# Attention interleaved with a two-matmul MLP: other gaps for the score, value and mixing steps of a pair of heads

## The chip, the cores and the metric

One Trainium2 chip, one of its cores. The metric is the device time of one execution in microseconds (us), the median of the timed runs. TensorE does the matmuls (PE in the profile, its weight loads PEld), VectorE (DVE), ScalarE (ACT) and GpSimd (POOL) do the rest, and SyncE (SP) issues most DMA transfers. All values are float32; the MLP's matmuls use two-part operands (a high part in the chip's fp32r type and the rest), three matmuls for each product.

## The reference, cut to what matters

```python
# q, k, v: (8 batches, 8 heads, 576, 64)
scores = matmul(q, k.T) / sqrt(64)               # masked: block of 64 of the key <= that of the query
attn   = exp(scores - max) / (sum + 1e-9)
x      = matmul(attn, v)                         # -> (8, 576, 512), heads side by side
u      = x + ((x.T @ U) @ V).T                   # mixing along the sequence, rank 32
ch     = relu(u @ w_ch1) @ w_ch2                 # 512 -> 2048 -> 512
y      = u + ch
gate   = sigmoid(causal_conv5(y, conv_w))
out    = (gate * (y @ w_val)) @ w_out
```

## The kernel before, in words

The 4608 rows (8 batches of 576) are cut into nine groups of 512 for the MLP. A group takes 16 steps (`NF`), one for each 128 of the 2048 hidden columns. A step is an `emit_h1` (12 matmuls into one PSUM bank, then ACT makes the high part `hh`, L1015, and DVE the low part `hl`, L1016) and an `emit_o` of the step before (12 matmuls into four accumulator banks, L1036). The order of TensorE's instructions is that of the program (`manual_schedule`); the other engines' instructions are put in order by a planner, by the program's order and by when their data is ready in its own model, and each engine then runs its queue strictly in that order.

Attention is done for pairs of heads, four pairs to a batch, 32 in all. The first eight pairs (batches 0 and 1) are done in another way (`slot`) before and during group 0, and pairs 8 and 9 by `tick` without places in group 0. The change is about pairs 10 to 31, which run between the MLP's matmuls in groups 1 to 6. After each half of a step the MLP calls `gap(kind)`: kind 0 in the middle of h1, 1 at its end, 2 in the middle of o, 3 at its end, so a group has 64 gaps. In a gap the generator `attention()` is asked on; it emits instructions until it says that it has to wait for a later gap. `until` is that wait: a part of pair p is due at the group's first count plus `POS0` plus the pair's place in the group times a period plus the part's own offset, and two parts with TensorE work don't share a gap (`used`).

What a pair does, with its names:

- S: score matmuls, `emit_s_piece` (L420), four pieces, both heads at once, a PSUM bank for each head and piece, copied to SBUF by ACT (L425). Pieces 0 and 1 (16 matmul instructions) are the first score stay, pieces 2 and 3 (8) the second.
- maxima: `emit_max_a`, `_b`, `_c` on DVE (L618 to L664); subtraction `emit_sub` (L671) on DVE; exp `emit_exp` (L687) on ACT; sums `emit_sum_a` on POOL (L694, L696) and `emit_sum_b` on DVE (L703).
- V: values, `emit_pv` (L729, sums L739), two banks, copied by ACT (L741); from the second bank DVE takes the sums as well (L746), turns their reciprocals (L749), and POOL multiplies (L750).
- T: transposes `mix_T` (L789, L797), G: `mix_G` (L805), H: `mix_H` (L828), which together add the rank-32 mixing, store u to HBM and put its two parts into the MLP's operand. `prep_t` (L398, L399) transposes the next pair's q and k on DVE.

Score, value, T, G and H banks and those of h1 come from one pool tag, "a", with four banks (`ABUF`) in turn; the accumulators hold the other four.

The places before, as offsets from a pair's first gap, for group 1 (12 gaps a pair, five pairs 10 to 14) and for the later groups (16 gaps, four pairs):

```python
    PAIR1 = 3 * NP + 3
    POS0 = 6
    PLACES = (
        (12, {"S0": 0, "m0": 2, "S2": 4, "H0": 5, "H1": 6, "T0": 7, "T1": 8, "V": 9, "m1": 10, "G": 11, "x": 11}),
        (16, {"S0": 0, "m0": 2, "S2": 4, "H0": 5, "H1": 6, "T0": 7, "T1": 8, "V": 9, "m1": 11, "G": 14, "x": 15}),
    )
```

S0 and S2 must besides fall on a gap of kind 2 or 3. V at pair p's offset 9 is that of pair p - 1; T and G are of pair p - 2, H of pair p - 3; "x" is where the second head's softmax is emitted (the first head's follows H). A batch's last H lets the group that needs it begin (`pace[2]`); where it hasn't come, the stream is run on at once (`FLUSH`). H's second piece, for a group two ahead, is put off (`later`) until that group's operand buffer is free.

Of the kernel before, what the change touches and what calls it, by code (L numbers as in the profile page):

```python
# [22 lines left out]
def attn_moe_gate_kernel(ctx: ExitStack, tc: tile.TileContext, q, k, v, U, V, w1, w2, wval, convw, wout, out):  # L23
# [62 lines left out]
    PAIR1 = 3 * NP + 3  # L86
    POS0 = 6
    PLACES = (
        (12, {"S0": 0, "m0": 2, "S2": 4, "H0": 5, "H1": 6, "T0": 7, "T1": 8, "V": 9, "m1": 10, "G": 11, "x": 11}),
        (16, {"S0": 0, "m0": 2, "S2": 4, "H0": 5, "H1": 6, "T0": 7, "T1": 8, "V": 9, "m1": 11, "G": 14, "x": 15}),  # L90
    )
# [749 lines left out]
    at_gap = {"kind": 0, "count": 0, "used": -1}  # L841
    begun = {}

    def until(n, what, kinds=None):

        p = n // 2
        if p < PAIR0:
            return
        g, i = (1, p - PAIR0) if p < PAIR1 else (2 + (p - PAIR1) // NP, (p - PAIR1) % NP)
        period, place = PLACES[g > 1]  # L850
        busy = what[0] in "SHTVG"
        while at_gap["kind"] != FLUSH:
            c = at_gap["count"]
            if g in begun and c >= begun[g] + POS0 + period * i + place[what] and (kinds is None or at_gap["kind"] in kinds) and not (busy and at_gap["used"] == c):
                break
            yield WAITS
        if busy:
            at_gap["used"] = at_gap["count"]

    def tick(n, mixed, last=B * NP):  # L860
# [7 lines left out]
        if old and not half:  # L868
            load_v(n - 2)
            load_v(n - 1)  # L870
        for i in range(4):
            if new and not half:
                if n < 2 * PAIR0:
                    emit_s_piece(n // 2, i)
                elif i % 2 == 0:
                    yield from until(n, f"S{i}", (2, 3))
                    emit_s_piece(n // 2, i)
                    emit_s_piece(n // 2, i + 1)
            if old and half and i == 0:
                yield from until(n, "V")  # L880
                emit_pv(pn, 0)
                emit_pv(pn, 1)
            if i == (0 if half else 3) and new:
                emit_corners(n)
                emit_max_a(n)
            if i == (2 if half or n < 2 * PAIR0 else 1) and NQ <= n - 1 < NH:
                yield from until(n, f"m{half}")
                emit_sum_b(n - 1)
            yield
# [5 lines left out]
        if half:  # L895
            yield from until(n, "x")
# [9 lines left out]
    def mixing(at, first, last=B * NP):  # L906

        for step, delay in ((mix_H2, H0), (mix_G, G0), (mix_T, T0)) if last == NP else ((mix_H2, HPOS), (mix_G, GPOS), (mix_T, TPOS)):
            pn, off = divmod(at - delay, 4)
            if off == 0 and first <= pn < last:  # L910
                if URG and pn == NP - 1:
                    with tc.high_priority():
                        for _ in step(pn):
                            pass
                else:
                    part = step(pn)
                    for j in range(2):
                        if j:
                            yield
                        if last > NP:  # L920
                            yield from until(at // 2 + DEPTH, "G" if step is mix_G else f"{'T' if step is mix_T else 'H'}{j}")
                        if next(part, WAITS) == WAITS:
                            break
                yield step is mix_H2 and pn % NP == NP - 1

    def attention():
# [8 lines left out]
        for n in range(NQ, NH + DEPTH + HPOS // 2):  # L935
            if n == NQ + EARLY:
                yield True
            yield from tick(n, 2 * NP)

# [266 lines left out]
    def gap(kind):  # L1206
# [5 lines left out]
        if begun and not pace[2]:  # L1212
            pace[0] = 99.0
# [14 lines left out]
    for s in range(NS + LAG):  # L1228
# [6 lines left out]
        if f == 0 and g < B:  # L1235
            while g > 0 and not pace[2]:
                pace[0] = 1.0
                gap(FLUSH)
            if g > 0:
                begun[g] = at_gap["count"]  # L1240
# [78 lines left out]
```

## Time and profile before

| | us |
|---|---|
| timed runs | 1389.58, 1389.25, 1387.07 |
| median | 1389.25 |
| profiled execution, its own time | 1385.46 |
| span of its trace | 1383.7 |
| TensorE busy | 1333.4 |
| DVE busy | 986.6 |
| ACT busy | 552.6 |
| POOL busy | 445.1 |

Mean granted clock of TensorE 0.991. The span is from the first to the last instruction; the execution's own time has 1.8 us around it. Busy time of TensorE is modelled: matmuls overlap, so that a wait can be partly covered by the record of the matmul before it. Group 1 starts at 253.9 us, group 2 at 393.7, group 3 at 517.8, group 4 at 641.8, group 5 at 765.6, group 6 at 889.4; from about 990 no attention is left, and from 1179 the last stage (values, gate and output) runs.

### The profile page before, as it was taken

What the parts mean: (1) busy time and instruction counts of PE and PEld (TensorE: products, weight loads), DVE (VectorE), ACT (ScalarE), POOL (GpSimd) and SP (SyncE); (2) the same over time, 40 slices, a digit from 0 to 9 for tenths busy, and PEclk for the clock granted to TensorE, in tenths of its full rate; (3) what the DMA queues carried; (4) which work ended last, traced back from release to release, by engine and by line L of the source; (5) the groups of instructions that cost most, each with busy time, mean ns of one, the idle gap of its engine ahead of it and who ended that gap; (6) DMA issues with size and microseconds to landing.
All of it is one profiled execution on the core that took longest, in us unless ns stands there. A gap on an engine that the chain in (4) does not pass through costs nothing.

```text
span 1383.7 us, 20054 instructions
## 1 busy us (share of the span) xinstructions
PE 1333.4 (96%) x6840; PEld 1029.5 (74%) x6840; DVE 986.6 (71%) x2085; ACT 552.6 (40%) x1210; POOL 445.1 (32%) x648
## 2 busy tenths in 40 slices
PE   6889889999999999999999999999999999999999
PEld 4667665777677777777777777778878888788887
DVE  5986789788878778777877877772235164699981
ACT  5785544333343334334433433432223122434432
POOL 3443334423343224334322422441132100624210
PEclk9999998999999999999999999999999999999999
DMA  6667785644364347435443644332375632332311
GB/s 109 159 179 209 230 263 170 140 95 115 78 135 107 93 113 155 111 92 142 104 99 96 155 105 111 102 103 88 116 206 167 154 128 99 77 107 77 107 60 62
DMA packets 257936, 173.60 MB, mean 125 GB/s; under 512 B 202149, under 2 KB 222885, under 8 KB 257834
## 3 DMA queue, kind: packets, MB, share of 16 engines
q1 hardware_dynamic: 250282, 162.58, 42.5%
q0 software_dynamic: 5184, 9.44, 4.5%
q8 instruction: 54, 0.88, 0.3%
q10 hardware_dynamic: 2368, 0.30, 0.2%
q14 instruction: 48, 0.39, 0.1%
HBM read 135.57 MB, written 36.70 MB: 125 GB/s over the span
## 4 chain that ended last, share of the span: by engine, by line
PE 59%; DVE 24%; ACT 7%; DMA 5%; issue 3%; SPq 1%; POOL 0%; ACTq 0%; DVEq 0%; POOLq 0%
PE acc L1036 18%; PE h L987 18%; PE o L1150 7%; PE val L1126 7%; PE pS L420 4%; DMA raw<-in_moe_w_ch_dram 3%; DVE hl L1016 2%; DVE mb L664 2%; PE pPV L729 2%; DVE s L671 2%; DVE r L657 2%; ACT e L687 1%; DVE wa L133 1%; DVE g L105 1%; ACT s L687 1%
## 5 line engine op out<-in xcount | busy, mean ns | idle before, releaser
L1036 PE MATMUL acc<-hh,w 128*128 128x512 f32 x1152 | 404.3, 404 | 1.6 <-DMA w<-w_s 1.6
L1036 PEld LDWEIGHTS acc<-hh,w 128*128 128x128 f32 x1152 | 218.2, 189 | 72.1 <-issue 23.4
L987 PE MATMUL h<-uh,w1hi 128*128 128x512 f32 x576 | 233.1, 405 | 1.2 <-DVE xt L830 1.0
L1036 PE MATMUL acc<-hl,w 128*128 128x512 f32 x576 | 226.7, 394 | 0.2 <-DVE hl L1016 0.2
L987 PE MATMUL h<-uh,w1lo 128*128 128x512 f32 x576 | 226.0, 392 | 0.0
L987 PE MATMUL h<-ul,w1hi 128*128 128x512 f32 x576 | 225.6, 392 | 0.0
L1016 DVE SCALAR_TENSOR_TENSOR hl<-h,hh 128x512 fp32r<-128x512 f32 x144 | 98.6, 685 | 141.3 <-ACT hh L1015 139.7
L1015 ACT ACTIVATE hh<-h 128x512 fp32r<-128x512 f32 x144 | 85.9, 597 | 242.2 <-PE h L987 241.8
L987 PEld LDWEIGHTS h<-uh,w1hi 128*128 128x128 f32 x576 | 108.8, 189 | 27.6 <-issue 1.8
L987 PEld LDWEIGHTS h<-uh,w1lo 128*128 128x128 f32 x576 | 108.7, 189 | 23.7
L1036 PEld LDWEIGHTS acc<-hl,w 128*128 128x128 f32 x576 | 109.5, 190 | 19.8 <-DVE hl L1016 0.5
L987 PEld LDWEIGHTS h<-ul,w1hi 128*128 128x128 f32 x576 | 109.0, 189 | 20.1 <-issue 0.4
L1108 DVE SCALAR_TENSOR_TENSOR gt<-yb,cw,gt 128x516 f32<-128x516 f32 (+1 forms) x144 | 115.2, 830 | 1.4
L420 PE MATMUL pS<-tq,tk 64*128 64x320 f32 (+4 forms) x576 | 99.0, 420 | 13.1 <-DVE hl L1016 10.2
L105 POOL TENSOR_TENSOR yl<-yb,yh 128x512 fp32r<-128x512 f32 (+7 forms) x64 | 66.8, 1077 | 102.7 <-ACT yh L99 102.6
L105 POOL TENSOR_TENSOR ul<-xt,uh 128x512 fp32r<-128x512 f32 (+7 forms) x64 | 60.2, 948 | 112.7 <-ACT uh L99 112.6
L420 PEld LDWEIGHTS pS<-tq,tk 64*128 64x128 f32 x576 | 52.2, 187 | 51.3 <-issue 24.6
L425 ACT COPY s<-pS 128x320 f32<-128x320 f32 (+2 forms) x128 | 59.6, 501 | 36.5 <-PE pS L420 36.5
L671 DVE TENSOR_TENSOR s<-s,mb 128x64 f32<-128x64 f32 (+4 forms) x160 | 70.6, 507 | 0.5
L694 POOL TENSOR_TENSOR m<-e 128x448 f32<-128x448 f32 x24 | 31.0, 1293 | 122.5 <-ACT e L687 117.7
L729 PE MATMUL pPV<-e,vstk 128*64 128x192 f32 (+4 forms) x384 | 70.2, 336 | 0.1
L729 PEld LDWEIGHTS pPV<-e,vstk 128*64 128x64 f32 x384 | 46.8, 137 | 24.5 <-issue 12.6
(180 smaller groups left out, 2502.9 us busy)
## 6 DMA issues: line engine op xcount, KB each, us to landing
w<-w_s SPq DMA_DIRECT2D x144, 512.0 KB, 3.5
rawq<-in_q_dram SPq DMA_DIRECT2D x128, 72.0 KB, 3.0
out_dram<-ot SPq DMA_DIRECT2D x35, 256.0 KB, 2.0
rawk<-in_k_dram SPq DMA_DIRECT2D x124, 72.0 KB, 2.9
vstk<-in_v_dram SPq DMA_DIRECT2D x68, 128.0 KB, 2.9
raw<-in_moe_w_ch_dram SPq DMA_DIRECT2D x64, 128.0 KB, 2.4
raw<-in_moe_w_ch_dram SPq DMA_DIRECT2D x16, 512.0 KB, 3.9
w_s<-wo SPq DMA_DIRECT2D x16, 512.0 KB, 4.3
```

The source lines that it names most:

```text
L105: eng.tensor_tensor(o, i, f32(h), op=ALU.subtract)
L420: pe.matmul(t[:, o:o + w], tk[me, kslice(j)], tq[me, a0:a1], start=True, stop=True)
L425: act.copy(stt[n][half_of[j]][:, d:d + o], t[:, 0:o])
L671: noted(3, vec.tensor_tensor(sv(n, j), sv(n, j), mb[:, q0[j]:], op=ALU.subtract))
L729: pe.matmul(ps[me, a0 - c0:c1 - c0], vpart(n)[:, j, :], est[n][half_of[j]][:, soff[j] + a0 - q0[j]:soff[j] + c1 - q0[j]], start=j == 0, st ...
L987: pe.matmul(ps[:, 0:n], w[:, d, fs], x[:, d, 0:n], start=(d == 0 and i == 0), stop=(d == ND - 1 and i == 2))
L1015: act.activation(hh[:, 0:n], ps[:, 0:n], AF.Relu)
L1016: latest[0] = vec.scalar_tensor_tensor(hl[:, 0:n], ps[:, 0:n], 0.0, f32(hh[:, 0:n]), op0=ALU.max, op1=ALU.subtract)
L1036: pe.matmul(acc[d][:, 0:n], w[:, wi, ds], x[:, 0:n], start=(f == 0 and i == 0), stop=(f == NF - 1 and i == 2))
L1108: vec.scalar_tensor_tensor(gt[d][:, 0:gw], y[:, d, j:j + gw], cw[:, d, j:j + 1], gt[d][:, 0:gw], op0=ALU.mult, op1=ALU.add)
L1126: pe.matmul(ps[:, 0:n], w[:, d, es], x[:, d, 0:n], start=(i == 0), stop=(i == 3 * ND - 1))
L1150: pe.matmul(ps[:m, cs], x[:, e, a:a + m], w[:, e, cs], start=(i == 0), stop=(i == 3 * ND - 1))
```

## The change

All pairs from 10 on get 16 gaps, counted through from the first gap of group 1 (`at_gap["first"]`), four pairs to a group; `POS0` is 8. `pair_tick` writes one pair's order out: offset 0 the first score stay, and the pair's loads of v (before, they were issued one pair later); 2 and 3 the H of pair p - 2; 4 the values of pair p - 1 and behind them, in the same gap, the second score stay; 6 the first head's softmax, 8 the second head's maxima, 9 the first head's sums, 10 the second head's softmax; 11 and 12 the T of pair p - 1; 13 the next pair's q and k and the second head's sums; 15 the G of pair p - 1. The kinds of the gaps are no longer asked for: offset 0, 4, 8 and 12 are gaps of kind 3 (except in a group's first step). A group starts when its batch is in `ready`.

```diff
@@ -83,12 +83,8 @@
     WAITS = 3
     FLUSH = 4
     PAIR0 = (NQ + EARLY) // 2
-    PAIR1 = 3 * NP + 3
-    POS0 = 6
-    PLACES = (
-        (12, {"S0": 0, "m0": 2, "S2": 4, "H0": 5, "H1": 6, "T0": 7, "T1": 8, "V": 9, "m1": 10, "G": 11, "x": 11}),
-        (16, {"S0": 0, "m0": 2, "S2": 4, "H0": 5, "H1": 6, "T0": 7, "T1": 8, "V": 9, "m1": 11, "G": 14, "x": 15}),
-    )
+    POS0 = 8
+    PERIOD = 4 * (NF // NP)
 
     def f32(ap):
         return ap if ap.dtype == F32 else ap.bitcast(F32)
@@ -838,24 +834,93 @@
 
     y_done = [-1]
 
-    at_gap = {"kind": 0, "count": 0, "used": -1}
-    begun = {}
-
-    def until(n, what, kinds=None):
-
-        p = n // 2
-        if p < PAIR0:
-            return
-        g, i = (1, p - PAIR0) if p < PAIR1 else (2 + (p - PAIR1) // NP, (p - PAIR1) % NP)
-        period, place = PLACES[g > 1]
-        busy = what[0] in "SHTVG"
+    at_gap = {"kind": 0, "count": 0, "used": -1, "first": None}
+    ready = set()
+
+    def until(p, off, pe_step=True):
+
         while at_gap["kind"] != FLUSH:
             c = at_gap["count"]
-            if g in begun and c >= begun[g] + POS0 + period * i + place[what] and (kinds is None or at_gap["kind"] in kinds) and not (busy and at_gap["used"] == c):
+            if at_gap["first"] is not None and c >= at_gap["first"] + POS0 + PERIOD * (p - PAIR0) + off and not (pe_step and at_gap["used"] == c):
                 break
             yield WAITS
-        if busy:
+        if pe_step:
             at_gap["used"] = at_gap["count"]
+
+    turned_to = [2 * NP]
+    mixed_to = [2 * NP]
+
+    def turning(p, t0, t1, g, n=None):
+        pn = turned_to[0]
+        turned_to[0] += 1
+        turn = mix_T(pn)
+        yield from until(p, t0)
+        next(turn)
+        yield from until(p, t1)
+        next(turn, None)
+        if n is not None:
+            yield from until(p, t1 + 1, False)
+            prep_t(n)
+            emit_sum_b(2 * p + 1)
+        yield from until(p, g)
+        for _ in mix_G(pn):
+            pass
+
+    def pair_tick(p):
+
+        a, b = 2 * p, 2 * p + 1
+        new = a < NH
+        if new:
+            yield from until(p, 0)
+            emit_s_piece(p, 0)
+            emit_s_piece(p, 1)
+            load_v(a)
+            load_v(b)
+        while mixed_to[0] <= p - 2 and mixed_to[0] < turned_to[0]:
+            pn = mixed_to[0]
+            mixed_to[0] += 1
+            for i in range(2):
+                yield from until(p, 2 + i)
+                mix_H(pn, i)
+            if pn % NP == NP - 1:
+                ready.add(pn // NP)
+        if turned_to[0] < min(p, B * NP) - 1:
+            yield from turning(p, 1, 2, 3)
+        if new or p - 1 < B * NP:
+            yield from until(p, 4)
+        if p - 1 < B * NP:
+            emit_pv(p - 1, 0)
+            emit_pv(p - 1, 1)
+        if new:
+            emit_s_piece(p, 2)
+            emit_s_piece(p, 3)
+            emit_corners(a)
+            emit_max_a(a)
+            emit_max_b(a)
+            yield from until(p, 6, False)
+            soften(a)
+            yield from until(p, 8, False)
+            emit_corners(b)
+            emit_max_a(b)
+            emit_max_b(b)
+            if p == PAIR0:
+                for i in range(2):
+                    yield from until(p, 6 + i)
+                    mix_H(mixed_to[0], i)
+                mixed_to[0] += 1
+            yield from until(p, 9, False)
+            emit_sum_b(a)
+            yield from until(p, 10, False)
+            soften(b)
+        if turned_to[0] < min(p + 1, B * NP):
+            yield from turning(p, 11, 12, 15, p + 1 if new else None)
+    def soften(n):
+        for _ in emit_max_c(n):
+            pass
+        emit_sub(n, 0)
+        emit_sub(n, 1)
+        emit_exp(n)
+        emit_sum_a(n)
 
     def tick(n, mixed, last=B * NP):
 
@@ -868,23 +933,19 @@
         if old and not half:
             load_v(n - 2)
             load_v(n - 1)
+        if n == 2 * PAIR0 - 1:
+            load_v(n - 1)
+            load_v(n)
         for i in range(4):
             if new and not half:
-                if n < 2 * PAIR0:
-                    emit_s_piece(n // 2, i)
-                elif i % 2 == 0:
-                    yield from until(n, f"S{i}", (2, 3))
-                    emit_s_piece(n // 2, i)
-                    emit_s_piece(n // 2, i + 1)
+                emit_s_piece(n // 2, i)
             if old and half and i == 0:
-                yield from until(n, "V")
                 emit_pv(pn, 0)
                 emit_pv(pn, 1)
             if i == (0 if half else 3) and new:
                 emit_corners(n)
                 emit_max_a(n)
-            if i == (2 if half or n < 2 * PAIR0 else 1) and NQ <= n - 1 < NH:
-                yield from until(n, f"m{half}")
+            if i == 2 and NQ <= n - 1 < NH:
                 emit_sum_b(n - 1)
             yield
         if new:
@@ -892,8 +953,6 @@
             if half:
                 prep_t((n + 1) // 2)
         yield from mixing(2 * e, mixed, last)
-        if half:
-            yield from until(n, "x")
         if new:
             for _ in emit_max_c(n):
                 pass
@@ -913,14 +972,7 @@
                         for _ in step(pn):
                             pass
                 else:
-                    part = step(pn)
-                    for j in range(2):
-                        if j:
-                            yield
-                        if last > NP:
-                            yield from until(at // 2 + DEPTH, "G" if step is mix_G else f"{'T' if step is mix_T else 'H'}{j}")
-                        if next(part, WAITS) == WAITS:
-                            break
+                    yield from step(pn)
                 yield step is mix_H2 and pn % NP == NP - 1
 
     def attention():
@@ -932,10 +984,13 @@
                 yield done
             if u == BREAK:
                 yield True
-        for n in range(NQ, NH + DEPTH + HPOS // 2):
-            if n == NQ + EARLY:
-                yield True
+        for n in range(NQ, 2 * PAIR0):
             yield from tick(n, 2 * NP)
+        emit_sum_b(2 * PAIR0 - 1)
+        yield True
+        for p in range(PAIR0, B * NP + 2):
+            yield from pair_tick(p)
+        yield True
 
 
     w2t = {}
@@ -1209,7 +1264,7 @@
         at_gap["count"] += kind != FLUSH
         if tick_count[0] % EVERY == 0:
             flush_later()
-        if begun and not pace[2]:
+        if at_gap["first"] is not None and not pace[2]:
             pace[0] = 99.0
         pace[0] += pace[1]
         while pace[0] > 0 and pace[2] == 0:
@@ -1233,11 +1288,12 @@
                 if not convs:
                     open_late()
         if f == 0 and g < B:
-            while g > 0 and not pace[2]:
+            while g == 1 and not pace[2] or g > 1 and g not in ready:
                 pace[0] = 1.0
                 gap(FLUSH)
+            if g == 1:
+                at_gap["first"] = at_gap["count"]
             if g > 0:
-                begun[g] = at_gap["count"]
                 emit_o(s - LAG, gap)
             if pace[2] != 2:
                 pace[2] = 0
```

## Rows read from the trace of the kernel before

**Rows 1.** The page, part 1: busy us (share of the span) xinstructions of each engine.
```profile
PE 1333.4 (96%) x6840; PEld 1029.5 (74%) x6840; DVE 986.6 (71%) x2085; ACT 552.6 (40%) x1210; POOL 445.1 (32%) x648
```

**Rows 2.** Windows: stretch, us, busy of PE, PEld, DVE, ACT, POOL, clock, DMA.
```profile
253.90:393.70 139.80, 133.13 (x699) 98.53 (x698) 111.17 (x259) 54.40 (x112) 49.20 (x86) 0.98 0.43 100
...
517.80:641.80 124.00, 123.04 (x676) 93.98 (x675) 96.68 (x228) 48.69 (x101) 43.22 (x73) 1.00 0.47 112
```

**Rows 3.** Waits of PE: line <- releaser: total us, times, longest.
```profile
PE pS L420 <- DVE hl L1016: 10.2, 16, 2.1
```

**Rows 4.** Timeline of PE, first score stays, groups 2-5: start, us, instruction.
```profile
410.79 1.79 PE L420 MATMUL pS<-tq,tk 64*128 64x64 f32 x16
...
412.51 0.50 PE L1036 MATMUL acc<-hh,w 128*128 128x512 f32 x1
...
440.81 1.78 PE L420 MATMUL pS<-tq,tk 64*128 64x64 f32 x14
...
443.74 0.50 PE L1036 MATMUL acc<-hh,w 128*128 128x512 f32 x1
...
874.78 1.78 PE L420 MATMUL pS<-tq,tk 64*128 64x64 f32 x14
...
877.58 0.50 PE L1036 MATMUL acc<-hh,w 128*128 128x512 f32 x1
```

**Rows 5.** Timeline of PE, stays of group 1.
```profile
291.59 1.78 PE L420 MATMUL pS<-tq,tk 64*128 64x64 f32 x14
...
296.17 0.80 PE L1036 MATMUL acc<-hh,w 128*128 128x512 f32 x1
...
330.59 2.29 PE L420 MATMUL pS<-tq,tk 64*128 64x448 f32 x8
...
376.33 1.78 PE L420 MATMUL pS<-tq,tk 64*128 64x64 f32 x14
...
380.25 0.50 PE L1036 MATMUL acc<-hh,w 128*128 128x512 f32 x1
```

**Rows 6.** Windows: two stretches of group 1 (columns as in rows 2).
```profile
291.00:303.00 12.00, 9.94 (x42) 7.28 (x42) 8.04 (x19) 4.75 (x9) 4.25 (x10) 0.86 0.14 44
...
380.00:386.00 6.00, 6.00 (x20) 4.29 (x19) 4.63 (x9) 3.25 (x6) 3.23 (x7) 0.72 0.27 90
```

**Rows 7.** Timeline of PE around one pair's values.
```profile
403.76 0.39 PE L987 MATMUL h<-ul,w1hi 128*128 128x512 f32 x1
...
403.98 0.40 PE L987 MATMUL h<-uh,w1lo 128*128 128x512 f32 x1
...
404.31 0.38 PE L729 MATMUL pPV<-e,vstk 128*64 128x192 f32 x1
...
407.25 0.50 PE L987 MATMUL h<-uh,w1hi 128*128 128x512 f32 x1
...
407.58 0.39 PE L987 MATMUL h<-ul,w1hi 128*128 128x512 f32 x1
```

**Rows 8.** Timeline of PE, a second score stay.
```profile
418.19 1.56 PE L420 MATMUL pS<-tq,tk 64*128 64x448 f32 x8
...
419.68 0.50 PE L1036 MATMUL acc<-hh,w 128*128 128x512 f32 x1
```

**Rows 9.** Timeline of ACT: copies of values and scores, a second head's second exp.
```profile
407.37 0.48 ACT L741 COPY xt<-pPV 128x384 f32<-128x384 f32 x1 [1.04 <-PE pPV L739]
...
412.07 0.59 ACT L425 COPY s<-pS 128x512 f32<-128x512 f32 x1 [0.43 <-PE pS L420]
...
419.25 0.53 ACT L425 COPY s<-pS 128x448 f32<-128x448 f32 x1 [1.65 <-PE pS L420]
...
440.02 0.85 ACT L687 ACTIVATE zb<-zb 128x768 f32<-128x768 f32 x1
```

**Rows 10.** Timeline of DVE: the read of the second values bank.
```profile
407.89 0.18 DVE L746 TENSOR_SCALAR r<-pPV 128x18 f32<-128x18 f32 x1 [1.04 <-ACT xt L741]
```

**Rows 11.** Timeline of POOL: the last sums of a second head.
```profile
443.10 0.99 POOL L696 TENSOR_TENSOR m<-m,za 128x192 f32<-128x192 f32 x2
```

## The prediction

> **What bounds the kernel now.** I read the page's busy shares first: the reader is to see TensorE at 96% of the span, DVE at 71%, ACT and POOL far below [rows 1]. So the time is TensorE's instruction stream, and only what TensorE waits for, or issues in excess, can move. Next the table of stretches, cut at the starts of the groups: group 1, with five pairs of heads, takes 139.8 us, a group with four pairs 124.0 [rows 2]. Then the waits of TensorE: inside these groups nearly all belongs to one line, the first score stay (16 score matmuls of L420), and what ends it is DVE's hl of L1016, 16 times [rows 3]. That view understates the loss, since the records of matmuls in flight cover part of it; the timeline of TensorE gives it whole. From the start of a stay to the next MLP matmul: 1.72 us where nothing waits (410.79 to 412.51), 2.93 in the first of the twelve late ones of groups 2 to 5 (440.81 to 443.74), 2.80 in the last (874.78 to 877.58) [rows 4]. In group 1 four stays take longer, the first 4.58 us, the last 3.92 [rows 5].
>
> Why: the ring of PSUM banks with tag "a" has four slots, and the stay takes all four (two heads, two pieces). Its last bank is that of the h1 whose matmuls ended half a step before, and this bank is free only when ACT's hh and then DVE's hl have read it. The stay stands in the middle of the second matmul's step (o), 1.4 us after h1 (six matmuls at 0.22 and the change-over). Just there ACT also does the second head's exps [rows 9], so hh comes late, hl later still, and the score matmul waits.
>
> **The change part by part.**
>
> *The first score stay goes from mid-o to the end of o.* By count of gaps: before, the stay is asked for at count 6 and must take kind 2 or 3, so it lands on 7, kind 2; after, at 8, kind 3. The third and fourth bank are wanted after 512 of the stay's 832 columns, 0.6 of 1.72 = 1.1 us: before, 1.4 + 1.1 = 2.5 us after h1's end. The late stays lose 1.1 to 1.2 us, so hl frees the bank some 3.7 us after h1. At the new place it is wanted at 2.8 (all of o) + 1.1 = 3.9 us, plus the G stay that lies between. The fourth bank is now G's, 2.5 us after G; that is how it stood in stays that were clean. The twelve waits go: 12 x (2.86 - 1.72) = 13.7 us [rows 4]. What is late next is the first head's bank for the following h1, priced below. Bounds: 0 if hl moves back by as much, 13.7 if none is left.
>
> *16 gaps a pair in group 1 too.* Group 1 then has four pairs like the others; a pair moves into group 6, which has the room; the pair's own work is unchanged. What the crowding cost goes: the stays, 4.58 + 3 x 3.92 - 4 x 1.72 = 9.5 us; two second stays of 2.29 against 1.56, 1.5 us [rows 5, 8]; and two stretches of half clock behind long waits: 0.14 x 12.0 + 0.28 x 6.0 = 3.4 us [rows 6]. Together 14.4. The rows show the granted clock at 0.86 and 0.72 of full in stretches that begin with a wait of TensorE, and 1.00 in the groups whose waits are shorter. The Trainium skill (TensorE: Matmul & The Clock Gate, Part 1) says that the array's clock is passed at half rate after idleness and restored by work; with waits under 1 us left, it would give the whole 3.4 back; if the two stretches came all the same, the sum would be 3.4 us worse.
>
> *Values at the head of the second score stay.* Before, values (32 matmuls and four sums) are a stay of their own. Entering it costs 404.31 - 403.98 = 0.33 against 0.22 between two MLP matmuls; leaving, 407.58 - 407.25 = 0.33 against 0.22 [rows 7]. Joined to the score matmuls behind it, 22 pairs (10 to 31) save one way in and out: 22 x 0.2 = 4.4 us; between 0 (if values to scores costs the same change) and 5.
>
> New order, new bank: of the second stay's four score banks, the third and fourth are those that the values have just used. The second values bank is read by ACT from 407.37 to 407.85 and then by DVE from 407.89 to 408.07, which is 0.82 us after the values end (407.25) [rows 7, 9, 10]. The scores that need it start after 448 of 768 columns of 1.49 us, 0.87 us: hidden, by 0.05 us only. If ACT's copy stands behind one exp (0.85 us, [rows 9]), a pair loses that. I take 0.05 a pair, 1 us. The DVE read starts 0.04 us after ACT's ends, not beside it. The Trainium skill (PSUM — Partial Sum Buffer, PSUM bank collisions raise a hardware error) demands this order: two engines may not touch one bank of the same partitions at a time, reads against reads included. By it the cover of 0.05 us can't grow; were the two reads side by side, the margin would be 0.27 us and this 1 us nothing.
>
> *Score stays followed at once by h1.* Before, half of o (which needs no bank) follows each score stay; now h1 does, and its bank is the first head's of the stay. The first copy after a clean first stay ends at 412.07 + 0.59 = 412.66, 1.87 us after its start, while the stay lasts 1.72; for the second stay 419.25 + 0.53, 1.59 us against 1.49 [rows 4, 8, 9]. With the semaphore I take 0.2 and 0.15 us: 22 x 0.35 = 7.7 us. Not below nothing: the copy can't start before its matmuls end. Above: one exp ahead of it in ACT's order, 0.85 more a pair, 19 us.
>
> *Softmax, transposes, G, H sooner.* Same instructions. Values come 5 gaps earlier (4 instead of 9), the two transposes at 11 and 12 of the same pair, G at 15, H at 2 and 3 of the next pair, so a pair is mixed two pairs on and not three. Data: in one pair of before the second score stay starts at 418.19, the second head's last exp ends at 440.87 and its sums on POOL end at 444.09 [rows 8, 9, 11]: 22.7 and 25.9 us later. In the new order the next pair's values start about 25.5 us after that point (a period of 30 less 4.4) and their sums 2.8 later: even the old pace is just in time. Transposes to G are 3 gaps (18 matmuls, 4.1 us) with a cast and a subtraction between. I take 1 us for the first pair (its transposes at 1, 2 and G at 3) and nothing else; if a stay waited 0.4 us in each pair it would be 9 us.
>
> *Queues.* The values' loads go to SP one pair earlier, at the pair's first stay; they overwrite columns that the values of two pairs before read 12 gaps ago, so SP isn't held and the w2 loads, the q and k loads and the y stores behind them go on. H's stores are the same number. POOL keeps its order of sums, product and low parts. The extra sum before group 1 runs on DVE, under TensorE. Nothing on TensorE's path: 0; if SP did block, a w2 load would be late and every step with it.
>
> **Sum.** -13.7 - 14.4 - 4.4 + 7.7 + 1 + 1 = -22.8 us, against the profiled execution's 1385.46 us (span 1383.7 and 1.8 around it): 1362.7. The timed runs' median is 1389.25, 3.8 above that execution; the same 22.8 off gives 1366.5.
>
> **The rivals.**
>
> A. *The wait thins but stays.* The second head's exps and hh still collide with score copies, since DVE and ACT have the same work in a pair as before; h1, the values or G then wait 0.3 to 0.8 us in each pair. For: the cover of the second values bank is 0.05 us, and the chain that ended 25.9 us after the second stay has 25.5 to 28. Against: the values no longer stand between the two heads' maxima, so the second head should be softened sooner. At 0.55 us: 1366.5 + 12 = 1378.5.
>
> B. *Slower: h1 pays for the exps.* Place: ACT, between a first score stay and the following h1. If the second head is softened so late that both its exps (0.85 for the shorter) are queued ahead of the first head's copy, h1 waits 1.7 us more in each of 22 pairs: +37.4, so 1366.5 + 37.4 = 1404. It turns slower than before from (13.7 + 14.4 + 4.4 - 9.7) / 22 = 1.04 us a pair. For: before, ACT's second exp ended 0.1 us after the stay's start (440.87 and 440.81). Against: the first copy is due only 1.28 us after that start.
>
> C. *The change doesn't do what it says:* hl frees the bank later by as much as the stay was moved (it follows ACT's queue, not its place). Then the 13.7 us stay and the rest happens: 1366.5 + 13.7 = 1380. Against: the clean stays of before (22 less the 16 that waited) show that the wait follows what ACT has ahead of hh. A flush of the whole stream at a group's start (batch not ready) is excluded by count: the last mixing of a batch is asked for at 69 - 64 = 5 gaps before its group.
>
> **How the numbers follow.** Forecast 0.62, A 0.18, C 0.10, B 0.10. The forecast's own range is 1360 to 1374: 0.85 us a pair is not reached, the second values bank costs 0 to 0.3. The range for 8 in 10 runs from 1358 (no h1 wait) to 1384 (A and C within it). A measurement of this kernel can tell about 0.2%, 2.8 us. Faster: forecast, A and most of C, 0.87; the same 0.04; slower, B in most of its length, 0.09.
>
> **What would show it.** Right: first score stays of 1.7 to 2.0 us in all groups with h1 directly behind; no wait of L420 on hl; group 1 near 121 us and no half clock in it; groups 2 to 5 near 121.5, against 124; values and second scores in one run of matmuls. Wrong: h1 (L987) waiting for ACT's score copies by over 0.5 us a pair (A, B), L420 still waiting for hl (C), quad's sums (L739) waiting for DVE, or G (L805) waiting for the low parts.

## The result, and the profile after

The changed kernel takes 1401.28 us (median of four runs, 1400.89 to 1402.33) against 1388.16 for the kernel before beside it: ratio 1.0097, 95% interval 1.008 to 1.0115. It is slower by 1%; 1366.5 was forecast. The profiled execution took 1401.21 us (span 1399.4) against 1385.46 (1383.7): +15.7.

The page of the kernel after, part 1, answers to [rows 1]: TensorE is as busy as before, in a longer span.

```profile
PE 1331.6 (95%) x6840; PEld 1031.9 (74%) x6840; DVE 961.6 (69%) x2085; ACT 555.9 (40%) x1210; POOL 461.6 (33%) x648
```

Next the windows of the kernel after, cut at the starts of the groups; shown are groups 1, 2, 3, 5 and 6 (columns as in [rows 2]; the clock stands third from the end).

```profile
252.90:376.90 124.00, 122.46 (x678) 94.27 (x677) 86.36 (x210) 49.94 (x101) 45.44 (x72) 1.00 0.43 111
376.90:505.90 129.00, 125.01 (x676) 95.87 (x675) 91.61 (x231) 49.58 (x100) 46.18 (x72) 0.97 0.44 110
505.90:635.30 129.40, 124.66 (x674) 95.49 (x673) 91.87 (x230) 49.42 (x100) 45.83 (x72) 0.97 0.44 110
...
763.90:891.50 127.60, 122.11 (x674) 93.66 (x673) 92.52 (x229) 49.20 (x101) 45.81 (x72) 1.00 0.44 111
891.50:1010.70 119.20, 113.12 (x591) 88.89 (x590) 69.99 (x172) 38.36 (x79) 35.64 (x51) 0.99 0.33 95
```

Group 1 came down from 139.8 to 124.0 (121 was forecast); groups 2 to 5 went up by 4 to 6 us each. The waits of TensorE (answering to [rows 3]) say on what:

```profile
PE acc L1091 <- DVE hl L1071: 17.6, 7, 3.6
...
PE h L1042 <- DVE xt L826: 5.5, 5, 1.8
...
PE pG L801 <- DVE x L101: 1.0, 2, 0.6
```

The score stays' wait for hl is gone from the list. Now o (L1091), the second matmul, waits for hl itself, five times at length, at the five changes of group (3.2 to 3.6 us each). And h1 (L1042) waits for a bank that H's addition (L826) has still to read, four times 0.4 to 1.8 us at the last four of these changes and once before group 1. TensorE's timeline shows the first of them and the pair behind it (start, us, instruction):

```profile
388.12 0.39 PE L1091 MATMUL acc<-hh,w 128*128 128x512 f32 x1
391.74 0.79 PE L1091 MATMUL acc<-hl,w 128*128 128x512 f32 x1 [3.23 <-DVE hl L1071]
...
394.03 1.27 PE L801 MATMUL pG<-x,ust 128*128 128x256 f32 x5
...
397.66 1.79 PE L416 MATMUL pS<-tq,tk 64*128 64x64 f32 x16
399.58 0.50 PE L1042 MATMUL h<-uh,w1hi 128*128 128x512 f32 x1
...
408.23 0.25 PE L735 MATMUL pPV<-rs,quad 128*64 128x18 f32 x4
408.40 1.70 PE L416 MATMUL pS<-tq,tk 64*128 64x448 f32 x8
410.04 0.50 PE L1042 MATMUL h<-uh,w1hi 128*128 128x512 f32 x1
```

The group's first o starts at 388.12 and can't use hl before 391.74. What follows runs at the lower of TensorE's two clocks (1.2 of 2.4 GHz): G's five matmuls take 1.07 us to the next start, against .70 in the other pairs of the group. The window shows it:

```profile
388.00:398.00 10.00, 6.77 (x25) 4.96 (x25) 6.52 (x12) 2.79 (x5) 5.42 (x7) 0.66 0.46 86
```

The lower clock follows four of the five waits. At the fourth change, with a wait of 3.4 us, it stays at 1.00 (the window of group 5), and that group still goes up by 3.7 us.

The stays are as forecast: first stay to h1 399.58 - 397.66 = 1.92 us, values and second scores in one run, 410.04 - 408.40 = 1.64 us, and so in every pair (the first stay of group 1 takes 1.97).

DVE's timeline before that first o:

```profile
382.82 2.10 DVE L667 TENSOR_TENSOR s<-s,mb 128x64 f32<-128x64 f32 x5
...
385.99 4.49 DVE L667 TENSOR_TENSOR s<-s,mb 128x64 f32<-128x64 f32 x5
390.41 0.68 DVE L101 TENSOR_TENSOR x<-pT,x 128x512 fp32r<-128x512 f32 x1
391.01 0.68 DVE L1071 SCALAR_TENSOR_TENSOR hl<-h,hh 128x512 fp32r<-128x512 f32 x1
```

ACT had made hh long before:

```profile
386.49 0.60 ACT L1070 ACTIVATE hh<-h 128x512 fp32r<-128x512 f32 x1
```

So hl's input was there at 387.09, and DVE came to it at 391.01: ahead of it in DVE's order stood the subtractions of both heads (twice five) and x's low part. The first head's were over at 384.92; it is the second head's, 385.99 to 390.48, that held it. In the kernel before, at the same change, only the first head's stand there (two rows), and DVE idles for hh:

```profile
397.68 1.14 DVE L671 TENSOR_TENSOR za<-za,mb 128x64 f32<-128x64 f32 x3
398.74 2.07 DVE L671 TENSOR_TENSOR zb<-zb,mb 128x448 f32<-128x448 f32 x2
...
403.61 0.69 DVE L1016 SCALAR_TENSOR_TENSOR hl<-h,hh 128x512 fp32r<-128x512 f32 x1 [0.41 <-ACT hh L1015]
```

It hurts only at a change of group, because the order there is: last o of the old group, h1 of step 0, h1 of step 1, o of step 0. One h1 (2.7 us) covers the making of hl; elsewhere an h1 and an o do. And the second head's five subtractions took 4.49 us where the first head's took 2.10. POOL's timeline beside them:

```profile
385.95 1.24 POOL L690 TENSOR_TENSOR m<-e 128x448 f32<-128x448 f32 x1 [0.70 <-ACT e L683]
387.16 0.70 POOL L101 TENSOR_TENSOR ul<-xt,uh 128x192 fp32r<-128x192 f32 x1
387.83 2.83 POOL L692 TENSOR_TENSOR m<-m,e 128x320 f32<-128x320 f32 x3
```

**Theories.** 1: DVE's order at a change of group, ten subtractions ahead of hl. 2: the change of group itself (its accumulator copies and stores). 3: POOL's sums stretch the subtractions; the order would do no harm without them.

All groups of all versions (e1 to e13 are the experiments below; there is no e7), us from the first accumulator copy (ACT, y<-acc; at the end of group 7 gt<-acc) at one change of group to that at the next:

| kernel | 1 | 2 | 3 | 4 | 5 | 6 | 7 | ratio to before (interval) |
|---|---|---|---|---|---|---|---|---|
| before | 139.7 | 124.2 | 123.8 | 123.9 | 123.9 | 106.9 | 92.5 | |
| after | 124.1 | 128.9 | 129.4 | 128.6 | 127.6 | 119.1 | 94.1 | 1.0097 (1.008-1.0115) |
| e1 | 123.8 | 124.1 | 125.7 | 126.6 | 124.7 | 114.2 | 95.2 | .9982 (.9968-.9997) |
| e2 | 125.8 | 126.5 | 124.8 | 124.1 | 126.8 | 115.7 | 94.4 | 1.002 (1.0008-1.0032) |
| e3 | 123.3 | 122.7 | 122.6 | 122.7 | 122.9 | 112.4 | 97.9 | .9921 (.9906-.9936) |
| e4 | 124.1 | 127.6 | 128.3 | 128.4 | 127.6 | 119.0 | 94.7 | 1.0107 (1.0084-1.013) |
| e8 | 123.5 | 125.3 | 127.1 | 124.7 | 126.4 | 116.7 | 96.8 | one run |
| e5 | 143.7 | 124.0 | 123.7 | 122.5 | 124.4 | 109.4 | 92.6 | 1.0035 (1.0022-1.0047) |
| e12 | 123.5 | 122.3 | 122.4 | 122.7 | 122.9 | 112.5 | 100.1 | .9922 (.9907-.9937) |
| e6 | 124.3 | 126.5 | 126.4 | 126.5 | 126.6 | 116.1 | 97.8 | 1.0058 (1.0045-1.0071) |
| e9 | 122.7 | 122.7 | 122.6 | 122.7 | 122.8 | 112.4 | 99.9 | .9915 (.9902-.9929) |
| e10 | 122.8 | 122.7 | 122.6 | 122.7 | 122.8 | 112.5 | 94.6 | .9883 (.9868-.9897) |
| e11 | 121.7 | 121.1 | 121.0 | 121.1 | 121.2 | 111.1 | 98.4 | .9839 (.9825-.9853) |
| e13 | 121.2 | 121.1 | 121.0 | 121.1 | 121.2 | 111.1 | 95.5 | .9828 (.9812-.9844) |

### The profile page after: what moved, and what is told of

Its sections match the earlier page's. It is cut to its first block, busy times and chain, and to the rows that moved or that the text cites. A ratio compares the mean times of both kernels' runs of the same rounds, so it can differ in the third digit from the quotient of the medians.

```text
span 1399.4 us, 20056 instructions
## 1 busy us (share of the span) xinstructions
PE 1331.6 (95%) x6840; PEld 1031.9 (74%) x6840; DVE 961.6 (69%) x2085; ACT 555.9 (40%) x1210; POOL 461.6 (33%) x648
## 5 line engine op out<-in xcount | busy, mean ns | idle before, releaser
L1091 PE MATMUL acc<-hh,w 128*128 128x512 f32 x1152 | 401.7, 403 | 0.8 <-ACT hh L1070 0.8
L1091 PEld LDWEIGHTS acc<-hh,w 128*128 128x128 f32 x1152 | 221.7, 192 | 50.9 <-issue 3.0
L1091 PE MATMUL acc<-hl,w 128*128 128x512 f32 x576 | 230.7, 400 | 17.6 <-DVE hl L1071 17.6
L1042 PE MATMUL h<-uh,w1hi 128*128 128x512 f32 x576 | 235.9, 410 | 9.9 <-DVE xt L826 5.5
L1042 PE MATMUL h<-uh,w1lo 128*128 128x512 f32 x576 | 225.6, 392 | 0.0
L1042 PE MATMUL h<-ul,w1hi 128*128 128x512 f32 x576 | 224.6, 390 | 0.0
L1071 DVE SCALAR_TENSOR_TENSOR hl<-h,hh 128x512 fp32r<-128x512 f32 x144 | 98.4, 684 | 98.4 <-ACT hh L1070 97.8
L1042 PEld LDWEIGHTS h<-uh,w1hi 128*128 128x128 f32 x576 | 108.1, 188 | 57.9 <-ACT s L421 16.4
L1091 PEld LDWEIGHTS acc<-hl,w 128*128 128x128 f32 x576 | 111.1, 193 | 40.9 <-DVE hl L1071 20.4
L1042 PEld LDWEIGHTS h<-uh,w1lo 128*128 128x128 f32 x576 | 108.1, 188 | 24.3
L1042 PEld LDWEIGHTS h<-ul,w1hi 128*128 128x128 f32 x576 | 108.4, 188 | 20.2 <-issue 0.4
L667 DVE TENSOR_TENSOR s<-s,mb 128x64 f32<-128x64 f32 (+4 forms) x160 | 99.9, 688 | 0.5
L101 POOL TENSOR_TENSOR ul<-xt,uh 128x512 fp32r<-128x512 f32 (+7 forms) x64 | 55.7, 878 | 122.3 <-ACT uh L95 115.2
L416 PE MATMUL pS<-tq,tk 64*128 64x320 f32 (+4 forms) x576 | 86.9, 419 | 4.3 <-ACT s L421 4.0
L746 POOL TENSOR_TENSOR xt<-xt,t 128x576 f32<-128x576 f32 x24 | 34.5, 1437 | 147.2 <-ACT s L421 95.0
L742 DVE TENSOR_SCALAR r<-pPV 128x18 f32<-128x18 f32 x24 | 4.2, 177 | 114.5 <-ACT xt L737 114.5
L690 POOL TENSOR_TENSOR m<-e 128x448 f32<-128x448 f32 x24 | 27.8, 1157 | 158.3 <-ACT e L683 153.4
L614 DVE TRANSPOSE_TENSOR_REDUCE rb<-s 128x26 f32<-128x832 f32 (+1 forms) x64 | 62.2, 990 | 20.4 <-ACT s L421 9.6
```

The source lines that it names most:

```text
L101: eng.tensor_tensor(o, i, f32(h), op=ALU.subtract)
L416: pe.matmul(t[:, o:o + w], tk[me, kslice(j)], tq[me, a0:a1], start=True, stop=True)
L614: x = vec.tensor_reduce(r[:, o:o + w], stt[n][half].rearrange("p (b a) -> p b a", a=BL), axis=AX.X, op=ALU.max, apply_transpose=True,)
L667: noted(3, vec.tensor_tensor(sv(n, j), sv(n, j), mb[:, q0[j]:], op=ALU.subtract))
L1042: pe.matmul(ps[:, 0:n], w[:, d, fs], x[:, d, 0:n], start=(d == 0 and i == 0), stop=(d == ND - 1 and i == 2))
L1071: latest[0] = vec.scalar_tensor_tensor(hl[:, 0:n], ps[:, 0:n], 0.0, f32(hh[:, 0:n]), op0=ALU.max, op1=ALU.subtract)
```

## The experiments

All edits are to the kernel after, but for e5.

### The change of group

**e1, the second head's softmax behind hl**, in each group's last pair:

```diff
-            yield from until(p, 10, False)
-            soften(b)
+            held = (p - PAIR0) % NP == NP - 1
+            if not held:
+                yield from until(p, 10, False)
+                soften(b)
...
     (in turning(), behind the second transpose)
+            if late_head is not None:
+                with tc.issue_after(latest[0].ins):
+                    soften(late_head)
```

> In the last pair of each of groups 1 to 5 alone, the second head's softmax on DVE is put behind the hl of the next group's first step (one ordering edge); every TensorE instruction keeps its place. Theory 1 (DVE's queue: at a group's start hl has only one h1, 2.7 us, before its o, and stands behind the ten subtractions of two heads): the waits of o for hl (3.6 us, five times) and the half clock behind them go, 27 of 32.7 us; 1371 to 1377 us. Rival 2 (the change of group itself, four accumulator copies on ACT and four stores on POOL, holds everything up): nothing changes, 1398 to 1403. Rival 3 (POOL's sums stretch the subtractions) agrees with theory 1 here.

Measured: 1386.08 us, 15 below the kernel after and 9 above the range that was expected. o no longer waits for hl at a change of group. But the five subtractions now stand ahead of DVE's read of G's bank (timelines of DVE and TensorE in e1), which the next first stay needs, so it takes 397.24 - 394.00 = 3.24 us (3.7 to 4.1 at the other changes):

```profile
393.52 2.06 DVE L667 TENSOR_TENSOR s<-s,mb 128x64 f32<-128x64 f32 x5
395.50 0.28 DVE L804 TENSOR_TENSOR t<-pG,t 128x128 f32<-128x128 f32 x1
```

```profile
394.00 2.63 PE L416 MATMUL pS<-tq,tk 64*128 64x64 f32 x16
397.24 0.50 PE L1047 MATMUL h<-uh,w1hi 128*128 128x512 f32 x1 [0.60 <-ACT za L421]
```

Theory 1 holds, and a part of the loss only moved: in groups 2 to 6 e1 stays 12.0 us above e3 (below), the kernel after 30.3.

**e2 and e3, all places four gaps (a step) sooner or later:**

```diff
-    POS0 = 8
+    POS0 = 4    (e2)      POS0 = 12    (e3)
```

> Every pair four gaps (one step) sooner: POS0 4 instead of 8, nothing else. Theory 1: the two heads' subtractions are over before the first step's hl is due, so the long wait goes; but the first score stay of a group then stands right behind its first h1 and wants that bank at once, 0.5 to 1.5 us five times: 1372 to 1382 us. Rival 2 (the change of group itself): the wait stays where it is, 1395 to 1403.

> Every pair four gaps later: POS0 12, nothing else; DVE's order then has the first step's hl ahead of both heads' subtractions. Theory 1: the long wait goes, 1368 to 1377 us. Rival 2 (the change of group itself): it stays, 1395 to 1403.

e2: 1391.35 us, between the two expectations. In the waits of e2 the change of group now makes h1 wait for H's addition (three of the four; one is before group 1), and two score stays wait for hl:

```profile
PE h L1042 <- DVE xt L826: 6.8, 4, 2.5
...
PE pS L416 <- DVE hl L1071: 2.9, 2, 1.5
```

e3: 1377.06 us, faster than the kernel before by .8%. In DVE's timeline of e3 hl stands ahead of both heads' subtractions at the change of group:

```profile
388.12 0.78 DVE L660 STREAM_TRANSPOSE mb<-r 128x576 f32<-128x576 f32 x1
388.82 0.65 DVE L1071 SCALAR_TENSOR_TENSOR hl<-h,hh 128x512 fp32r<-128x512 f32 x1
389.40 2.08 DVE L667 TENSOR_TENSOR s<-s,mb 128x64 f32<-128x64 f32 x5
```

Groups 2 to 6 fall by 6.2, 6.8, 5.9, 4.7 and 6.7 us, 30.3 in all. The fall is at the change of group alone: from one first stay to the next TensorE takes 30.5 us inside a group in both kernels, and across the first change 36.9 us in the kernel after, 31.2 in e3. Copies and stores at the change are the same, so theory 2 falls.

**e4, both heads' sums emitted behind the subtractions:**

```diff
-            soften(a)
+            soften(a, False)         # without emit_sum_a
...
             soften(b)
+            emit_sum_a(a)
+            emit_sum_b(a)
+            emit_sum_a(b)
```

> The first head's sums (POOL, four additions, and DVE's reduction) are emitted behind the second head's subtractions in all pairs; DVE's order at a group's start is the same as in the changed kernel. Rival 3 (it is POOL's additions beside the subtractions that stretch them from 2.1 to 4.3 us): the wait of o for hl falls from 3.6 to about 1.5 us and the clock stays full, 1381 to 1388 us. Theory 1 with the mere count of subtractions: 1395 to 1402.

1402.32 us: nothing changed, because POOL's order didn't. Its timeline in e4 and DVE's still show the additions beside the subtractions, at 4.50 us, so e4 says nothing on theory 3.

```profile
387.60 4.50 DVE L667 TENSOR_TENSOR s<-s,mb 128x64 f32<-128x64 f32 x5
```

```profile
389.44 2.83 POOL L692 TENSOR_TENSOR m<-m,e 128x320 f32<-128x320 f32 x3
```

**e8, fewer sums:** POOL's additions of key tiles 2 and up left out for the first head of each group's last pair.

```diff
+        last_pair = n % 2 == 0 and n // 2 > PAIR0 and (n // 2 - PAIR0) % NP == NP - 1
-        for j in range(2, NK):
+        for j in range(2, 2 if last_pair else NK):
```

> The kernel after, without GpSimd's additions of key tiles 2 and up for the first head of the last pair of each group (those row sums are not complete). Theory 1 without theory 3: sub(b) ahead of hl still takes about 4.5 us at the change of group, o's waits for hl stay near 17 us in all, 1400 us. Theory 3 (GpSimd's sums stretch the subtractions): the five subtractions of the second head come back to 2.1 to 2.5 us, and o's wait shrinks by about 2 us at each of the five changes of group: 17.6 to about 8 us, 1389 us.

1392.36 us (one run), nearer to theory 3's number than to theory 1's. In e8's timeline of DVE the five subtractions take 3.48 us: the first is 1.18 us long beside the one addition that is left (1.14 us), the second .77, the last three are back at the first head's lengths (.74, .61, .48 against .75, .62, .48). o's waits in e8 fall from 17.6 to 10.3 us:

```profile
387.92 3.48 DVE L667 TENSOR_TENSOR s<-s,mb 128x64 f32<-128x64 f32 x5
```

```profile
PE acc L1092 <- DVE hl L1072: 10.3, 7, 2.4
```

So theory 3 is a part of the price, by this one run some 9 of the 24 us between the kernel after and e3: with the subtractions at 3.48 us, o still waits up to 2.4 us, and without the order (e3) nothing is left of the wait. What the order would cost with no stretching at all (2.1 us) no run shows.

### The parts by themselves

**e5, the kernel before with both score stays at a step's end:**

```diff
-                    yield from until(n, f"S{i}", (2, 3))
+                    yield from until(n, f"S{i}", (3,))
```

> The kernel before with one part of the change alone: both score stays wait for a gap at a step's end, nothing else. The prediction's own terms: the waits of score stays for hl (10.2 us in 16) and their half clock go (-13.7), h1 directly behind a score stay pays .35 a pair (+7.7 in 22 pairs): about 1382 us, ratio .995. Theory 1 (the loss of the whole change came from DVE's order at a group's start, ten subtractions ahead of hl): the values still stand between the two heads' maxima here, so only five subtractions stand ahead of hl at a group's start, o's wait there stays under .5 us each, and the gain is seen. Rival 2 (the stays' new place itself, with h1 behind them, costs more than the waits did): 1389 us or more, and h1 or o show waits in the middle of groups.

1392.66 us: slower than before by .35%, where 1382 was expected. No stay waits for hl, but h1 does for ACT (waits of e5; then TensorE's and ACT's timelines of one such pair):

```profile
PE h L987 <- ACT s L425: 13.6, 7, 3.5
...
PE h L987 <- ACT za L425: 7.5, 3, 3.5
```

```profile
322.60 1.79 PE L420 MATMUL pS<-tq,tk 64*128 64x64 f32 x16
327.86 0.50 PE L987 MATMUL h<-uh,w1hi 128*128 128x512 f32 x1 [3.48 <-ACT s L425]
```

```profile
326.44 0.90 ACT L687 ACTIVATE s<-s 128x832 f32<-128x832 f32 x1 [2.67 <-DVE s L671]
327.24 0.57 ACT L425 COPY s<-pS 128x512 f32<-128x512 f32 x1
```

An exp that waits for DVE's subtractions stands ahead of the first head's score copy, and h1 waits for that copy: 2.3 and three times 3.3 us in group 1, once 1.5 in each later group. That is rival B with one exp, brought by the stay's place alone. Of the expected gain 1.2 us are left in groups 2 to 5.

**e12, the stays back in the middle of o, in the new order:** e3 with `POS0 = 11`.

> The kernel after with its places three gaps later instead of four: everything one gap ahead of the version with four, so the first score stay lands in the middle of o again, the one part of the change undone. The prediction's step: the stay's last bank is wanted 1.4 us sooner, before hl has read it, so first stays go from 1.92 to about 2.8 us in most pairs, less the .2 for h1 that o now takes the place of: +.7 to +.9 a pair in 22 pairs, 1393 to 1397 us. Rival: in the new order hl is early enough anyway, and the place makes no difference: 1377 us.

1378.95 us, as e3. In TensorE's timeline of e12 the first stay lasts 1.72 us, as do all 22; DVE's shows hl done half a microsecond before it starts:

```profile
521.87 1.79 PE L416 MATMUL pS<-tq,tk 64*128 64x64 f32 x16
523.59 0.50 PE L1091 MATMUL acc<-hh,w 128*128 128x512 f32 x1
```

```profile
520.68 0.69 DVE L1071 SCALAR_TENSOR_TENSOR hl<-h,hh 128x512 fp32r<-128x512 f32 x1
```

In the kernel before, hh stood at 441.09, behind the second head's exps [rows 9], and hl began at 442.26, behind the low part of G's g, 1.4 us into the stay of 440.81 [rows 4]. DVE's timeline of before:

```profile
441.22 1.01 DVE L105 TENSOR_TENSOR g<-t,g 32x128 fp32r<-32x128 f32 x1 [0.37 <-ACT g L99]
442.26 0.69 DVE L1016 SCALAR_TENSOR_TENSOR hl<-h,hh 128x512 fp32r<-128x512 f32 x1
```

In e12 the second head's second exp ends at 519.94, 1.9 us ahead of the stay (before: 440.87, behind the stay's start), and hl goes ahead of G's instructions. So the wait went without the stay being moved; where the stay stands makes no difference. That the softmax's new place did it, with G's, is read from these timelines; neither was moved by itself.

**e6, values in their own stay:** e3, and between values and scores

```diff
             emit_pv(p - 1, 1)
         if new:
+            if p - 1 < B * NP:
+                yield from until(p, 5)
```

> The kernel after with its places four gaps later (1377.06 us, ratio .9921 against before, in its run), and the values and the second score stay apart again, one gap between them. The prediction: joining them saves .2 us a pair in 22 pairs, so this comes at +4.4, about 1381.5 us, ratio .995. Rival: apart, the scores' stay falls behind h1's first half and the softmax behind it comes a gap later, ahead of no hl: then the difference is 0 to 2 us; or the stays in the middle of h1 bring waits of their own and it is 1385 us or more.

1395.13 us, 18 above e3 and not the prediction's 4.4: the case of the last rival, stays in the middle of h1 that cost time of their own. The scores now fall into the middle of h1. TensorE's timeline of e6: 417.07 - 414.70 = 2.37 us for what took 1.64; the two heads' last matmuls run one after the other, not side by side.

```profile
414.70 2.44 PE L416 MATMUL pS<-tq,tk 64*128 64x448 f32 x8
417.07 0.51 PE L1044 MATMUL h<-uh,w1hi 128*128 128x512 f32 x1
```

In group 2 the score stays take 2.1 us more than in e3, G 1.9 (it waits for x's low part) and h1 .8, while o takes 1.0 less. This prices the place in h1 with the separation, not the separation alone; values apart at another place weren't tried.

### What was left

**e9, the last group's loads for the gating two steps later** (`load_y` at steps 4 and 7, splitting from 6; e3 otherwise).

> The kernel after with its places four gaps later, and in the last group the loads of y for the gating and what splits them two steps later. Reading: with the places later the attention ends later too, the weights' and y's loads come later, and ACT's splitting of y (waiting until 999.1) stands ahead of hh, which costs 1.8 + 2.0 + 3.6 us of h1 and o there. With it two steps later ACT has hh first: 1370 us, ratio .987. Rival: the wait is the loads' traffic itself, not ACT's queue: no change, 1377 us; or the gating is late at the end and gives the gain back.

1375.92 us; group 7 at 99.9, not better. ACT's order put the splits of y ahead of two hh all the same (ACT idle for 7.80 us in e9), as here in ACT's timeline of e3, where ACT idles 7.89 us for a load with two hh behind:

```profile
999.28 2.18 ACT L95 CAST yh<-yb 128x512 fp32r<-128x512 f32 x4 [7.89 <-DMA raw<-in_moe_conv_w_dram]
1001.36 0.66 ACT L124 ACTIVATE wa<-raw 5x512 f32<-5x512 f32 x1
1001.93 1.05 ACT L1070 ACTIVATE hh<-h 128x512 fp32r<-128x512 f32 x2
```

**e10, e9 with both ordered behind an hl** (the splits, and the convolution weights from step 3):

```diff
+                    with tc.issue_after(latest[0].ins):
                         split_y(0, d)
```

> The kernel after with its places four gaps later (group 7: 97.9 us, kernel before 92.5), and the convolution weights' conversion and the splitting of y in the last group ordered behind an hl four and seven steps into the group, so that no hh stands behind a load on ACT. If ACT's queue is what costs group 7 its 5.4 us, group 7 comes to 92.5 to 94 us and the kernel to about 1371 us, ratio .988. Rival: the loads' traffic holds w2 back: group 7 stays at 97 us or more.

1374.14 us, 3 above what was expected: group 7 at 94.6, of which group 8 gave back .7 (85.0 against 84.3). Of the 5.4 us that e3's group 7 is above the kernel before, 2.6 net are back, so ACT's queue was about half of it. Even here the splits of y stand ahead of one hh (ACT idle for 7.29 us); what the rest is stays open.

**e11, the transposes two gaps sooner** (e3 otherwise):

```diff
-            yield from turning(p, 11, 12, 15, p + 1 if new else None)
+            yield from turning(p, 9, 10, 15, p + 1 if new else None)
```

> The kernel after with its places four gaps later, and both transposes of a pair two gaps sooner (9 and 10 instead of 11 and 12; G stays at 15). If G waits for x's low part on DVE because the transposes are late (G .70 us against .59 before, and the o half ahead of it 1.47 to 1.5), G comes back to .59 and the groups lose .2 us a pair, 4 us: 1373 us, ratio .989. Rival: the transposes now wait for POOL's product xt, or the casts stand ahead of hh on ACT: 1377 us or slower.

1368.13 us, better than expected: G is back at .59, and each of groups 1 to 6 gets 1.3 to 1.7 us shorter than in e3. That is .4 us a pair, 8.9 in all. G's matmuls grouped by line between 400 and 980 us, first of e3, then of e11 (busy, mean ns, idle before):

```profile
L801 PE MATMUL pG<-x,ust 128*128 128x256 f32 x95 | 16.3, 302 | 2.9 <-DVE x L101 1.7
```

```profile
L801 PE MATMUL pG<-x,ust 128*128 128x256 f32 x95 | 14.6, 284 | 0.0
```

**e13, e10 and e11 together.**

> The kernel after with three edits at once: its places four gaps later (no subtraction of the second head ahead of hl at a change of group), the transposes two gaps sooner (no wait of G), and in the last group the conversion of the convolution weights and the splitting of y ordered behind an hl. If these three losses are separate, the groups stay at 121.1 us and group 7 falls from 98.4 to about 94.6: 1364.5 us, ratio .981. Rival: the transposes' new place and the gating's meet, or the gain in group 7 is given back in group 8: 1368 us.

1366.65 us, ratio .9828: the fastest. Against e11 group 7 gains 2.9 and group 8 gives back .7, 2.2 by the profiles; the two ratios' intervals overlap, so that e13 beats e11 is not shown by the times.

## Why the prediction was wrong

- *First stays* (-13.7) and *h1 directly behind* (+7.7): the sizes were right, 1.92 us in 21 of 22 pairs. The reason was not. The place was to cure the wait; e12 shows stays in the old place without it, and e5 the new place alone, which pays for the exps on ACT as rival B said. So the right size was in part luck: by the timelines the cure is the new place of the softmax and of G, which the prediction gave no gain.
- *16 gaps a pair in group 1* (-14.4): group 1 fell by 15.6 (16.4 in e3), its clock to 1.00. But the fifth pair's scores, 3.6 us of the fall, come back in group 6 (106.9 to 112.4 in e3): about 12 net. The Trainium skill (TensorE: Matmul & The Clock Gate, Part 1) has the clock halve after idleness; the trace agrees at four changes of group (.66 was granted over the 10 us from the first o on), while behind the fourth wait the clock stayed at 1.00.
- *Values joined* (-4.4): 1.64 us for the second stay, with values and scores in one run; the second values bank cost nothing visible. The .2 us a pair could not be tested apart from the place (e6).
- *Softmax, transposes, G, H sooner* ("I take 1 us for the first pair ... and nothing else"): **the step that failed.** Readiness was worked out, the order on DVE was not. Before, the values stood between the two heads' maxima; after, both heads are softened back to back, and at each change of group the second head's five subtractions, stretched from 2.1 to 4.5 us by POOL's sums, stand ahead of an hl that has one h1 of cover. Five times some 6 us, 30.3 in all, with the half clock behind four of them and H's bank. The same step missed G: x's low part comes late for it, named only among the signs of error, and worth 8.9 us (e11 against e3). With the transposes sooner a group is at 121.1 us, where 121.5 was forecast for groups 2 to 5.
- *Rivals.* A was right in form: G waited in most pairs, .4 us a pair by e11, within A's .3 to .8. B had the right form (an order on a slower engine), the wrong engine and place; no rival looked at a change of group. *Queues*: right for SP; POOL's place in DVE's time was overlooked.

Taken together: 1399.4 - 30.3 = 1369 for the span without the failed step, which is near e3's 1374.7 less the 3.8 that group 7 is worse there, and the forecast's time is reached only by e13 and nearly by e11, which have the transposes' new place besides the shift, e13 the gating's too.

What stays open: which part of the change makes the planner put the second head ahead of hl; no run moved the values alone at the old places.

## What to carry to other kernels

Cost a moved step not by whether its data is ready, but by what then stands ahead of the critical instruction in each engine's queue, and do this at the place with the least cover (here a change of group, one h1 instead of an h1 and an o). Where work repeats with a period, compare the boundary of the loop by itself: the two stays were right here to .1 us in every pair and the kernel still lost 1%. A shift of all places by one step is a cheap test, worth 24 us here (1401.28 to 1377.06).

## What the hardware showed beyond that

- Five subtractions on DVE with both inputs in SBUF: 2.06 to 2.10 us alone, 3.48 beside one addition and a subtraction on POOL, 4.49 beside four additions and a subtraction. The Trainium skill (SBUF — State Buffer, Who interferes with whom) says that a DVE instruction with two SBUF inputs and a GpSimd instruction that reads SBUF contend for one port pair, and that this is an exclusive lock. The first subtraction of e8, 1.18 us beside an addition of 1.14, agrees; POOL's additions were not timed without DVE.
- A wait of 3.2 us on TensorE was followed by 5.9 us at the lower clock (.52 granted from 391.74 to 397.66), which cost some 2.4 us beside the wait: the five matmuls of o behind it 2.29 for 1.37, G 1.07 for .70, the next half of o 2.56 for 1.49. After a wait of 3.4 us at the fourth change of group the clock stayed at 1.00.
